# Moving a Q/K piece ahead of the second memory half, regrouping deferred rows around PV, deferring V-row stores, and using free banks at stage two, in a recurrent attention and spatial-gating kernel

## Chip, cores and metric

One core of a Trainium2 chip. The metric is device time in microseconds (us), lower is better. The runs of one kernel spread by up to 0.9% here, so small effects are read from distances inside a trace; the best of these repeat to about 0.002 us. With one core there is no second die to compare, so a run counts as fast unless it is over 1.5% above the fastest of its kernel.

Engines: PE is TensorE, ACT is ScalarE, DVE is VectorE, POOL is GpSimd, SP issues most DMAs.

## The reference

```python
x = A_x                                   # 2048 rows of 512
h = x + A(layernorm(x), mem0, Wq, Wk, Wv, Wo)   # 64 segments of 32 rows, 8 memory rows
h2 = h + B(layernorm(h), w_in, w_sp, b_sp, w_out)

def A(x, mem, ...):                       # 32 heads of 128
    for s in range(64):
        h = concatenate([mem, x[32*s:32*s+32]])          # 40 rows
        q, k, v = h @ Wq, h @ Wk, h @ Wv                 # per head
        p = softmax(mask(q @ k.T * 128 ** -0.5))
        o = (p @ v) @ Wo                                 # summed over heads
        mem = o[:8]                                      # the next segment needs it
        out.append(o[8:])

def B(x, ...):
    z = gelu(x @ w_in);  z1, z2 = halves(z)
    g = w_sp @ layernorm(z2) + b_sp
    return (z1 * g) @ w_out
```

What matters is the recurrence. The eight memory rows of a segment come out of its output projection, and the next segment's Q, K and V all need them. So 64 segments run one after the other, and anything that lengthens the chain inside a segment is paid 64 times.

## The kernel before

The kernel has three stages: weights arrive and the first projections are made (about 55 us), 64 segments follow (about 620 us), and the dense part B ends it (about 175 us). The change touches all three. Eight of the 32 rows of each segment (here "extra" rows) have their Q, K and V, which do not depend on the memory, computed beforehand in batches and kept. Their output projection is deferred too, as no later segment needs it: the "batched rows" of the change are groups of four such matmuls, taken from a queue and used as filler. (The prediction calls them "deferred memory-row products". That is a slip: the memory rows' own projection cannot be deferred, and `cTx`, which these matmuls read, holds the extra rows. Its argument does not depend on it.)

PSUM has eight banks:

```python
# (half of the heads, first pair, pairs, 0 = Q / 1 = K, PSUM bank)
QKP = ((0, 0, 8, 0, 0), (0, 0, 8, 1, 1), (1, 0, 8, 0, 6), (1, 0, 4, 1, 7), (1, 4, 4, 1, 2))
SB = 5                                  # scores
UBK = (0, 1)                            # softmax sums
PVB = (0, 1, 6, 7)                      # PV
VB = {(0, 0): 6, (1, 0): 7, (1, 2): 2}  # V: its first half goes to bank 6
OB = 2; OB2 = 6                         # output projection, first and second 256 columns
Tst = sb("Tst", [128, 2, 512], BF)      # staging: one slot for Q, one for K

def QK(s, k, dc, first=0, last=3, held=False):   # four matmuls, one per column tile of 32
    b, p0, np_, mi, bank = QKP[k]
    ...
def QK_evac(piece):
    b, p0, np_, mi, bank = piece
    st_ = Tst[:, mi, 64 * p0:64 * (p0 + np_)]
    tok = [("T", mi, k) for k in halves(b, p0, np_)]
    act(... st_ <- ps[:, bank, 0:64 * np_] ..., reads=[PB(bank)], writes=tok)     # ACT copy
    dve(... QT or KT <- transpose(st_) ..., reads=tok, ...)                       # DVE transpose
```

One segment, in the order in which PE gets its work:

```python
QK(s, 0, 0); QK(s, 1, 0, last=2, held=True)
if s > 0:
    mem_out(s - 1, 1)                   # second memory half: columns for dc 2 and 3
QK(s, 0, 1); QK(s, 1, 1, last=2, held=True)
QK(s, 0, 2); QK(s, 0, 3);               QK_evac(QKP[0])    # first piece: Q of heads 0..15
QK(s, 1, 3, last=2, held=True)
QK(s, 1, 2, last=2);                    QK_evac(QKP[1])    # second: K of the same heads
QK(s, 2, 2, first=2, last=0, held=True)
QK(s, 2, 3, first=2, last=0)
QK(s, 2, 1, first=2, last=0)
QK(s, 2, 0, first=2, last=0);           QK_evac(QKP[2])    # third: Q of heads 16..31
...                                                        # fourth and fifth: K of those
S_half(s, 0)                            # scores: needs the first and second piece transposed
sm_exp(0)
for dc in range(DC): V_half(s, 0, (0, 4), dc)              # V, first half, into bank 6
... sm_sums(0) ... S_half(s, 1) ... V_half(s, 1, ...) ... sm_sums(1) ...
nw1, nw2, nw4 = (2, 1, 2, 1)[j4], 0, 1  # fillers: before PV, after PV, at the end; j4 = s % 4
fill(nw1); xs[:2]; PV_half(s, 0); PV_half(s, 1); xs[2:4]; fill(nw2)
Wo(WOQ, OB, 0, OC);     part_evac(s, OB, 0, OC)
Wo(WOQ[:6], OB2, OC, D)
mem_out(s, 0)                           # first memory half: columns for dc 0 and 1
Wo(WOQ[6:], OB2, OC, D); part_evac(s, OB2, OC, D)
fill(nw4)
```

In the first stage each of eight V-row groups of 128 KB goes to memory at once, on the GpSimd queue, while Wk and Wo still arrive on the SP queue:

```python
t, tok = part[:, n, :], ...             # ck == 0
em.add("pool", lambda e: e.dma_start(dst, t...), reads=tok, writes=[("vext", ck, n)], dma=True)
```

At the entry of part B (the change calls it stage two), the last deferred products go to bank 4 (`WXB`), behind F_group in bank 3 (`XB`), and z1 of part B follows.

The softmax here doesn't subtract the row's maximum and nothing guards it: scores larger than these inputs give would overflow.

## Time and profile before

| | before |
|---|---|
| median time, all four runs of the first comparison | 854.16 us (852.58 to 854.69) |
| profiled span | 848.4 us, clock 0.999 |
| first output-projection matmul of segment zero | 54.57 us |
| first memory half ready to start (L722, first) | 57.04 us |
| period of segments without filler | 9.723 us |
| period with filler, odd / even segments, median | 9.724 / 9.751 us |
| last segment's first output-projection matmul | 671.33 us |
| from there to the end | 177.07 us |

The period is the distance from one segment's first output-projection matmul to the next one's. It is the number to watch: 63 periods make 600 us, so 0.1 us in each is 6.3 us.

The prediction shows the lines of this profile that it rests on. In such lines the columns are start, time busy, engine, line, operation, output and input, shape and number, and in brackets how long the engine sat idle and for whom.

```profile
148.11 0.60 ACT L559 ACTIVATE f_Tst<-f_ps 128x512 bf16<-128x512 f32 x1 [0.21 <-PE f_ps L289]
148.86 0.20 PE L601 MATMUL f_ps<-f_QT,f_arena 128*32 128x64 bf16 x4
148.89 1.03 PE L289 MATMUL f_ps<-f_arena,f_hT 128*32 128x512 bf16 x16
```

V (L289, the sixteen matmuls at 148.89) writes bank 6. The same bank holds the third Q/K piece until that ACT copy ends, at 148.71. V follows the last score matmuls (L601) by 0.03 us: it waits for nothing.

The same stretch of segment zero, where no memory has to be waited for and the pieces come bunched, looks different:

```profile
49.09 0.28 PE L595 MATMUL f_ps<-f_QT,f_KT 128*32 128x40 bf16 x16 [0.30 <-DVE f_KT L567]
49.21 0.20 PE L601 MATMUL f_ps<-f_QT,f_arena 128*32 128x64 bf16 x4
49.30 1.05 PE L289 MATMUL f_ps<-f_arena,f_hT 128*32 128x512 bf16 x16
```

Here S waits for the K transpose, and V comes 0.09 us after L601, not 0.03.

### The profile page before, as it was taken

The page shows a single profiled execution, that of the slowest core. Times are in us where ns is not written, and L with a number is a line of the kernel's source. Part 1 is how long each engine was busy: PE and PEld are TensorE (multiplying, and loading weights), DVE is VectorE, ACT ScalarE, POOL GpSimd, SP SyncE. Part 2 cuts the span into 40 slices and gives each one's busy share as a digit, 9 for nine tenths or more (in the row PEclk, how much of TensorE's full clock was granted, in tenths as well). Part 3 has the DMA queues.
Part 4 walks back from the last instruction along what each step waited for, and adds up shares of the span by engine and source line. Part 5 has one row for each costly group of instructions (what it writes and reads, how often), then busy time and mean ns, then how long its engine had stood idle before and what let it go on. Part 6 is the DMA issues. An engine that isn't in the chain of part 4 may idle for free.

```text
span 848.4 us, 46072 instructions
## 1 busy us (share of the span) xinstructions
PE 834.1 (98%) x22552; PEld 438.3 (52%) x19480; DVE 515.3 (61%) x1322; ACT 471.7 (56%) x1367; POOL 168.7 (20%) x425
## 2 busy tenths in 40 slices
PE   8889999999999999999999999999999999999998
PEld 8545555555545555555555555555555544444443
DVE  3456666676666666666766666666666664453443
ACT  3446666766667676667666666767666755300000
POOL 7312212121212122221222121122111232100000
PEclk9999999999999999999999999999999999999999
DMA  9972220222332221322222324242321690033001
GB/s 319 392 231 75 69 74 28 60 72 61 77 92 58 50 66 43 75 38 61 60 73 73 95 57 80 60 94 72 58 52 56 188 280 7 1 112 106 32 12 40
DMA packets 112920, 75.25 MB, mean 89 GB/s; under 512 B 70728, under 2 KB 98512, under 8 KB 112720
## 3 DMA queue, kind: packets, MB, share of 16 engines
q1 hardware_dynamic: 111504, 70.88, 30.2%
q8 instruction: 166, 2.72, 1.3%
q0 software_dynamic: 384, 1.05, 0.3%
q10 hardware_dynamic: 832, 0.33, 0.1%
q14 instruction: 34, 0.28, 0.1%
HBM read 39.46 MB, written 20.58 MB: 71 GB/s over the span
## 4 chain that ended last, share of the span: by engine, by line
PE 92%; SPq 5%; DMA 1%; issue 0%; DVE 0%; ACT 0%
PE f_ps L289 33%; PE f_ps L701 14%; PE f_ps L290 12%; PE f_ps L1172 11%; PE f_ps L751 3%; PE f_ps L666 3%; PE f_ps L1165 3%; PE f_ps L1248 3%; SPq L329 3%; PE f_ps L1129 3%; PE f_ps L498 2%; DMA f_arena<-in_A_Wo_dram 1%; SPq L825 1%; PE f_ps L595 1%; PE f_ps L615 1%; PE f_ps L672 1%
## 5 line engine op out<-in xcount | busy, mean ns | idle before, releaser
L289 PE MATMUL f_ps<-f_arena,f_hT 128*32 128x512 bf16 (+1 forms) x5632 | 359.7, 331 | 0.3
L289 PEld LDWEIGHTS f_ps<-f_arena,f_hT 128*32 128x32 bf16 x5632 | 133.1, 96 | 161.6 <-issue 69.8
L290 PE MATMUL f_ps<-f_arena,f_hT 128*32 128x512 bf16 (+1 forms) x2560 | 188.5, 315 | 0.0
L559 ACT ACTIVATE f_Tst<-f_ps 128x512 bf16<-128x512 f32 (+1 forms) x320 | 149.7, 510 | 57.6 <-PE f_ps L289 53.9
L701 PE MATMUL f_ps<-f_arena,f_cT 128*32 128x256 bf16 x4096 | 130.6, 274 | 0.9 <-DMA f_arena<-in_A_Wo_dram 0.6
L638 POOL TENSOR_TENSOR f_E_sb<-f_R_sb,f_E_sb 128x64 bf16<-128x64 f32 x128 | 57.0, 446 | 362.1 <-ACT f_R_sb L630 362.1
L567 DVE STREAM_TRANSPOSE f_QT<-f_Tst 128x256 uint32<-128x256 uint32 x128 | 57.1, 446 | 94.3 <-ACT f_Tst L559 94.3
L701 PEld LDWEIGHTS f_ps<-f_arena,f_cT 128*32 128x32 bf16 x4096 | 90.0, 94 | 37.1 <-ACT f_cT L686 23.2
L1172 PE MATMUL f_ps<-f_arena 128*128 128x512 bf16 x448 | 100.6, 379 | 0.0
L688 DVE TENSOR_SCALAR f_cT<-f_ps 128x160 bf16<-128x160 f32 x256 | 65.2, 318 | 35.2 <-PE f_ps L672 35.2
L713 ACT ACTIVATE f_part<-f_ps 128x256 bf16<-128x256 f32 x128 | 49.1, 383 | 57.7 <-PE f_ps L701 53.7
L658 DVE TENSOR_SCALAR f_V_sb<-f_ps 128x512 bf16<-128x512 f32 (+1 forms) x128 | 71.1, 555 | 13.6 <-PE f_ps L289 13.6
L686 ACT ACTIVATE f_cT<-f_ps 128x160 bf16<-128x160 f32 x256 | 57.1, 310 | 36.3 <-PE f_ps L672 36.3
L1172 PEld LDWEIGHTS f_ps<-f_arena 128*128 128x128 bf16 x448 | 43.8, 98 | 52.8
L567 DVE STREAM_TRANSPOSE f_KT<-f_Tst 128x128 uint32<-128x128 uint32 (+1 forms) x192 | 65.9, 356 | 2.8
L626 ACT ACTIVATE f_R_sb<-f_ps 128x160 f32<-128x160 f32 x128 | 38.9, 304 | 34.8 <-PE f_ps L290 34.8
L634 DVE TENSOR_TENSOR f_E_sb<-f_R_sb,f_E_sb 128x160 bf16<-128x160 f32 x128 | 41.7, 326 | 23.4 <-ACT f_R_sb L630 23.4
L1178 DVE TENSOR_TENSOR f_arena<-f_ps,f_arena 128x512 f32<-128x512 f32 x28 | 19.3, 690 | 54.4 <-PE f_ps L1172 52.4
L289 PE MATMUL f_ps<-f_arena,f_hTe 128*32 128x512 bf16 x640 | 48.8, 382 | 0.0
L608 ACT ACTIVATE f_E_sb<-f_ps 128x224 bf16<-128x224 f32 x128 | 45.9, 359 | 0.1
L751 PE MATMUL f_ps<-f_arena,f_cTx 128*32 128x512 bf16 x512 | 43.9, 379 | 0.5 <-issue 0.4
L630 ACT ACTIVATE f_R_sb<-f_R_sb 128x160 f32<-128x160 f32 x128 | 42.6, 332 | 2.0
(123 smaller groups left out, 1027.3 us busy)
## 6 DMA issues: line engine op xcount, KB each, us to landing
wT_d<-f_wst SPq DMA_DIRECT2D x32, 256.0 KB
f_arena<-wT_d SPq DMA_DIRECT2D x32, 256.0 KB
f_arena<-in_A_Wv_dram SPq DMA_DIRECT2D x4, 1024.0 KB
f_arena<-in_A_Wk_dram SPq DMA_DIRECT2D x4, 1024.0 KB
f_arena<-in_A_Wo_dram SPq DMA_DIRECT2D x4, 1024.0 KB
f_Vx<-vext_d SPq DMA_DIRECT2D x124, 32.0 KB
f_arena<-in_A_Wq_dram SPq DMA_DIRECT2D x3, 1024.0 KB
vext_d<-f_Vs SPq DMA_DIRECT2D x20, 128.0 KB
```

The costliest lines, as they stand in the source:

```text
L289: return e.matmul(out, lhsT=lhsT, rhs=rhs, start=start, stop=stop, skip_group_check=True, tile_position=pos)
L290: return e.add_instruction(mybir.InstMatmult(name=nc.get_next_instruction_name(), engine=mybir.EngineType.PE, ins=[e.lower_ap(rhs), e.lowe ...
L559: act(lambda e: e.activation(out=st_.rearrange("p (hp i r) -> p hp i r", i=32, r=2), in_=ps[:, bank, 0:64 * np_].rearrange("p (hp r i) -> ...
L567: dve(lambda e: e.transpose(out=dst, in_=src), reads=tok, writes=[(nm, b, k) for k in halves(b, p0, np_)])
L638: pool(lambda e: e.tensor_tensor(out=ev, in0=rv, in1=ev, op=ALU.mult), reads=[("R", b), ("Ex", b)], writes=[("Ex", b)])
L658: dve(lambda e: e.tensor_scalar(out=dst, in0=src, scalar1=VSC, scalar2=None, op0=ALU.mult), reads=[PB(bank)], writes=tok)
L686: act(lambda e: e.activation(out=dst, in_=src, func=ACT.Copy, scale=UNSC), reads=[PB(PVB[c])], writes=tok)
L688: dve(lambda e: e.tensor_scalar(out=dst, in0=src, scalar1=UNSC, scalar2=None, op0=ALU.mult), reads=[PB(PVB[c])], writes=tok)
L701: pe(lambda e, h=h, g=g, i=i, b=b, c=c: e.matmul(ps[32 * g:32 * g + 32, bank, 0:d1 - d0], lhsT=cTh[:, i, 8:40], rhs=w_o[:, h, d0:d1], star ...
L713: act(lambda e: e.activation(out=part[:, s % 8, d0:d1], in_=ps[:, bank, 0:d1 - d0], func=ACT.Copy), reads=[PB(bank)], writes=[("part", s % ...
L751: pe(lambda e, h=h, g=g, i=8 * qr + bg: e.matmul(ps[32 * g:32 * g + 32, WXB, :], lhsT=cTx[:, rb % 2, i, :], rhs=w_o[:, h, :], start=(i < 4 ...
L1172: pe(lambda e: e.matmul(ps[:, bank, 0:TB], lhsT=z2[:, sc, fb * 128:(fb + 1) * 128], rhs=wTb[tb % 2][:, :, sc, :], start=(sc == 0), stop=(s ...
```

## The change

Its intent, in four parts: (1) fewer DMA bytes while the weights arrive: most V rows are stored in segments two and three (counting from one), and segment zero's output projection takes the last quarter of Wo last; (2) two groups of the third Q/K piece, which need only the first memory half, run ahead of the second memory half, so that PE does not wait for it; (3) the filler of the segment's end moves to before and after PV; (4) the deferred products at stage two's entry use banks 1 and 0, which are free.

```diff
 def vx_evac(ck, n, bank, eng="act", q="sp"):                     # (1)
-    if ck == 1 and n < 4: ... hbuf, xo
-    elif ck == 0: t, tok = part[:, n, :], ...
+    if ck == 0: t = (hbuf, xo, Vs, wst2)[n // 2][:, n % 2, :] ...
+    elif ck == 1 and n < 4: ... part[:, (n + 3) % 4 + 4, :] ...
 ...
+    def store(q, p0, p1):
+        em.add(q, lambda e: e.dma_start(dst[p0:p1], src[p0:p1]), reads=tok, dma=True, ...)
+    elif q == "pool": store(q, 0, 32)               # only 32 of 128 partitions at once
+    return lambda: store("sp", 32 if q == "pool" else 0, 128)
 ...
+    for n in (4, 5): stores[0, n]()                 # behind Wo
+    if s == 1: for n in (6, 7, 0, 1, 2, 3): stores[0, n]() ; stores[1, 0]()
+    if s == 2: for n in range(1, 4): stores[1, n]()
 ...
+    if s == 0:                                      # last quarter of Wo used last
+        q0 = [(c, b) for b in range(2) for c in range(4)]
+        for i, d0 in ((0, 0), (1, 0), (0, OC), (1, OC), (2, 0), (2, OC), (3, 0)): Wo(q0[2*i:2*i+2], ...)

-    OB2 = 6                                                       # (2)
+    OB2 = 7
     QK(s, 0, 0); QK(s, 1, 0, last=2, held=True)
+    QK(s, 2, 0, last=3, held=True)
     mem_out(s - 1, 1)
     QK(s, 0, 1); QK(s, 1, 1, last=2, held=True)
+    QK(s, 2, 1, last=3, held=True)
     ...
-    QK(s, 2, 2, first=2, last=0, held=True); QK(s, 2, 3, ...); QK(s, 2, 1, ...); QK(s, 2, 0, ...)
+    QK(s, 2, 2, held=True); QK(s, 2, 3)
     ... (fourth and fifth piece in the order 3, 1, 2, 0 instead of 0, 1, 2, 3)

-    nw1, nw2, nw4 = (2, 1, 2, 1)[j4], 0, 1                        # (3)
+    nw1, nw2, nw4 = 2, (1, 0, 1, 0)[j4], 0

-    F_group(RB - 1, XB); for qr in range(4): WoX_mm(RB - 1, qr)   # (4)
+    for qr in range(4): WoX_mm(RB - 1, qr, bank=1)
+    F_group(RB - 1, 0)
```

More of the change, by code (lines that the diff above doesn't have):

```diff
@@ L246, in fast_path @@
     wst = sb("wst", [128, RB, 64], BF)
+    wst2 = wst[:].rearrange("p r c -> p (r c)").rearrange("p (j f) -> p j f", j=2)
     ident = sb("ident", [128, 128], BF)
@@ L502, in vx_evac @@
     def vx_evac(ck, n, bank, eng="act", q="sp"):
-        if ck == 1 and n < 4:
-            t, tok = (hbuf, xo)[n // 2][:, n % 2, :], [(("h", "xo")[n // 2], n % 2)]
-        elif ck == 0:
-            t, tok = part[:, n, :], [("part", n, 0), ("part", n, 1)]
+        if ck == 0:
+            t = (hbuf, xo, Vs, wst2)[n // 2][:, n % 2, :]
+            tok = [(("h", "xo", "Vs", "wst")[n // 2], n % 2)]
+        elif ck == 1 and n < 4:
+            i = (n + 3) % 4 + 4
+            t, tok = part[:, i, :], [("part", i, 0), ("part", i, 1)]
         else:
@@ L513, in vx_evac @@
         dst = vext_d[ck, n // 4, 2 * (n % 4):2 * (n % 4) + 2, :, :].rearrange("g p f -> p g f")
-        if q is not None:
-            em.add(q, lambda e: e.dma_start(dst, t.rearrange("p (g f) -> p g f", g=2)), reads=tok, writes=[("vext", ck, n)], dma=True)
-        return lambda: sp(lambda e: e.dma_start(dst, t.rearrange("p (g f) -> p g f", g=2)), reads=tok, writes=[("vext", ck, n)])
+        src = t.rearrange("p (g f) -> p g f", g=2)
+        def store(q, p0, p1):
+            em.add(q, lambda e: e.dma_start(dst[p0:p1], src[p0:p1]), reads=tok, dma=True,
+                   writes=[("vext", ck, n, i) for i in range(2) if p0 <= 32 * i < p1])
+        if q == "sp":
+            store(q, 0, 128)
+        elif q == "pool":
+            store(q, 0, 32)
+        return lambda: store("sp", 32 if q == "pool" else 0, 128)
     def load_vx(s, q="sp"):
@@ L522, in load_vx @@
             em.add(q, lambda e, b=b, src=src: e.dma_start(Vx[:, s % NVX, b, :], src),
-                   reads=[("vext", s // CK, n) for n in range(4 * b, 4 * b + 4)], writes=[("Vx", s % NVX, b)], dma=True)
+                   reads=[("vext", s // CK, n, int(s % CK > 3)) for n in range(4 * b, 4 * b + 4)], writes=[("Vx", s % NVX, b)], dma=True)
     QKP = ((0, 0, 8, 0, 0), (0, 0, 8, 1, 1), (1, 0, 8, 0, 6), (1, 0, 4, 1, 7), (1, 4, 4, 1, 2))
@@ L694, in fast_path, with Wo @@
     WOQ = ((0, 0), (2, 0), (0, 1), (2, 1), (1, 0), (3, 0), (1, 1), (3, 1))
-    def Wo(cbs, bank, d0, d1):
+    def Wo(cbs, bank, d0, d1, first=WOQ[0], last=WOQ[-1]):
         for c, b in cbs:
@@ L701, in Wo @@
                 pe(lambda e, h=h, g=g, i=i, b=b, c=c: e.matmul(
-                    ps[32 * g:32 * g + 32, bank, 0:d1 - d0], lhsT=cTh[:, i, 8:40], rhs=w_o[:, h, d0:d1], start=((c, b) == WOQ[0]),
-                    stop=((c, b) == WOQ[-1]), tile_position=(0, 32 * g)),
+                    ps[32 * g:32 * g + 32, bank, 0:d1 - d0], lhsT=cTh[:, i, 8:40], rhs=w_o[:, h, d0:d1], start=((c, b) == first),
+                    stop=((c, b) == last), tile_position=(0, 32 * g)),
                     reads=[("cT", c, b), ("Wo", h // 8)], writes=[PB(bank)])
@@ L745, in load_h, with WoX_mm @@
         sp(lambda e: e.dma_start(hbuf[:, rb % 2, :], xr[:, rb, :]), writes=[("h", rb % 2)])
-    def WoX_mm(rb, qr, bgs=range(8)):
+    def WoX_mm(rb, qr, bgs=range(8), bank=WXB):
         for bg in bgs:
@@ L750, in WoX_mm, with WoX_evac @@
             h = 16 * b + 4 * qr + g
-            pe(lambda e, h=h, g=g, i=8 * qr + bg: e.matmul(ps[32 * g:32 * g + 32, WXB, :], lhsT=cTx[:, rb % 2, i, :], rhs=w_o[:, h, :],
+            pe(lambda e, h=h, g=g, i=8 * qr + bg: e.matmul(ps[32 * g:32 * g + 32, bank, :], lhsT=cTx[:, rb % 2, i, :], rhs=w_o[:, h, :],
                                                            start=(i < 4), stop=(i >= H - 4), tile_position=(0, 32 * g)),
-               reads=[("cTx", rb % 2), ("Wo", h // 8)], writes=[PB(WXB)])
-    def WoX_evac(rb):
-        act(lambda e: e.activation(out=partx[:], in_=ps[:, WXB, :], func=ACT.Copy), reads=[PB(WXB)], writes=["partx"])
+               reads=[("cTx", rb % 2), ("Wo", h // 8)], writes=[PB(bank)])
+    def WoX_evac(rb, bank=WXB):
+        act(lambda e: e.activation(out=partx[:], in_=ps[:, bank, :], func=ACT.Copy), reads=[PB(bank)], writes=["partx"])
     def WoX_scatter(rb, bank):
@@ L794, in wT_piece @@
     def wT_piece(i):
-        sp(lambda e: e.dma_start_transpose(out=wst[:, :, :], in_=B_w_sp[i * 64:(i + 1) * 64, :]), writes=["wst"])
-        sp(lambda e: e.dma_start(wT_d[i], wst[:, :, :]), reads=["wst"], writes=[("wTd", i)])
+        tok = [("wst", 0), ("wst", 1)]
+        sp(lambda e: e.dma_start_transpose(out=wst[:, :, :], in_=B_w_sp[i * 64:(i + 1) * 64, :]), writes=tok)
+        sp(lambda e: e.dma_start(wT_d[i], wst[:, :, :]), reads=tok, writes=[("wTd", i)])
     act(lambda e: e.preload_act_table_set("natural_log_exp_and_others"))
@@ L836, in start_group @@
         return ev(*a, bk, "act" if cnt % 2 == 0 else "dve")
-    stores = []
+    stores = {}
     def start_v(ck, n):
-        if ck == 0:
-            start_group(vx_mm, lambda *a: vx_evac(*a, q="pool"), ck, n)
-        else:
-            stores.append(start_group(vx_mm, lambda *a: vx_evac(*a, q=None), ck, n))
+        stores[ck, n] = start_group(vx_mm, lambda *a: vx_evac(*a, q=None if ck else "pool"), ck, n)
     for i in range(2, 8):
@@ L874, in fast_path @@
         load_vx(j, "act")
-    for f in stores:
-        f()
+    for n in (4, 5):
+        stores[0, n]()
     gx = []
@@ L939, in fast_path @@
             load_h(rb - 1)
+        if s == 1:
+            for n in (6, 7, 0, 1, 2, 3):
+                stores[0, n]()
+            stores[1, 0]()
+        if s == 2:
+            for n in range(1, 4):
+                stores[1, n]()
         if s % 2 == 1 and s // 2 < NWT:
@@ L962, in fast_path @@
         QK_evac(QKP[1])
-        QK(s, 2, 2, first=2, last=0, held=True)
-        QK(s, 2, 3, first=2, last=0)
-        QK(s, 2, 1, first=2, last=0)
-        QK(s, 2, 0, first=2, last=0)
+        QK(s, 2, 2, held=True)
+        QK(s, 2, 3)
         lastop["q"] = em.by_eng["pe"][-1]
         QK_evac(QKP[2])
-        QK(s, 3, 0, held=True)
-        QK(s, 4, 0, last=2, held=True)
-        QK(s, 3, 1)
-        QK(s, 4, 1, last=2, held=True)
-        QK(s, 3, 2)
-        QK(s, 3, 3)
+        QK(s, 3, 3, first=3, last=0, held=True)
+        QK(s, 4, 3, first=3, last=2, held=True)
+        QK(s, 3, 1, first=3, last=0)
+        QK(s, 4, 1, first=3, last=2, held=True)
+        QK(s, 3, 2, first=3, last=0)
+        QK(s, 3, 0, first=3, last=0)
         QK_evac(QKP[3])
-        QK(s, 4, 3, last=2, held=True)
-        QK(s, 4, 2, last=2)
+        QK(s, 4, 0, first=3, last=2, held=True)
+        QK(s, 4, 2, first=3, last=2)
         lastop["k"] = em.by_eng["pe"][-1]
@@ L1051, in fast_path @@
             f()
-        Wo(WOQ, OB, 0, OC)
-        part_evac(s, OB, 0, OC)
-        Wo(WOQ[:6], OB2, OC, D)
+        if s == 0:
+            q0 = [(c, b) for b in range(2) for c in range(4)]
+            for i, d0 in ((0, 0), (1, 0), (0, OC), (1, OC), (2, 0), (2, OC), (3, 0)):
+                Wo(q0[2 * i:2 * i + 2], OB2 if d0 else OB, d0, d0 + OC, q0[0], q0[-1])
+            part_evac(s, OB, 0, OC)
+        else:
+            Wo(WOQ, OB, 0, OC)
+            part_evac(s, OB, 0, OC)
+            Wo(WOQ[:6], OB2, OC, D)
         if s + 1 < NSEG:
@@ L1057, in fast_path @@
             mask_dve()
-        Wo(WOQ[6:], OB2, OC, D)
+        if s == 0:
+            Wo(q0[6:], OB2, OC, D, q0[0], q0[-1])
+        else:
+            Wo(WOQ[6:], OB2, OC, D)
         cTx_copy(s)
@@ L1199, in fast_path @@
         if rb == 0:
-            F_group(RB - 1, XB)
             for qr in range(4):
-                WoX_mm(RB - 1, qr)
+                WoX_mm(RB - 1, qr, bank=1)
+            F_group(RB - 1, 0)
             endA = em.by_eng["pe"][-1]
-            WoX_evac(RB - 1)
+            WoX_evac(RB - 1, 1)
             load_wT(1, [endA])
@@ L1207, in fast_path @@
         if rb == 2:
-            WoX_scatter(RB - 1, XB)
-            F_add(RB - 1, XB)
+            WoX_scatter(RB - 1, 0)
+            F_add(RB - 1, 0)
             h_done(RB - 1)
```

## The prediction

> **What bounds it now.** The clock and the shares come first. The granted clock is full throughout, and the page says that TensorE (PE) is busy for almost the whole span.
>
> ```profile
> PE 834.1 (98%) x22552; PEld 438.3 (52%) x19480; DVE 515.3 (61%) x1322; ACT 471.7 (56%) x1367; POOL 168.7 (20%) x425
> PE 92%; SPq 5%; DMA 1%; issue 0%; DVE 0%; ACT 0%
> ```
>
> Matmul ends are modelled, so 98% does not say that PE has no slack. I therefore read distances from start to start in the timeline of PE. The kernel has three stages: about 55 us in which weights arrive, 64 recurrent segments, and about 175 us of dense work. The segments decide. From the first output-projection matmul (L701) of one segment to that of the next it is 9.72 us in the first four segments, which carry no batched rows (the deferred memory-row products L751, L736, L761). It is also 9.72 to 9.76 us in later ones, which carry two or three groups of four such matmuls of 0.216 us. So 0.4 to 0.6 us of work costs nothing: a dependency chain sets the period, and the batched rows sit in its holes. The two holes are these. First the tail, without filler (segment two) and with it (segment ten):
>
> ```profile
> 76.48 0.21 PE L722 MATMUL f_ps<-f_G_sb,f_part 128*32 128x8 bf16 x8
> 76.55 0.39 PE L701 MATMUL f_ps<-f_arena,f_cT 128*32 128x256 bf16 x8
> 77.00 0.40 PE L289 MATMUL f_ps<-f_arena,f_hT 128*32 128x512 bf16 x4
> ...
> 144.67 0.21 PE L722 MATMUL f_ps<-f_G_sb,f_part 128*32 128x8 bf16 x8
> 144.74 0.39 PE L701 MATMUL f_ps<-f_arena,f_cT 128*32 128x256 bf16 x8
> 144.96 0.39 PE L751 MATMUL f_ps<-f_arena,f_cTx 128*32 128x512 bf16 x4
> 145.19 0.40 PE L289 MATMUL f_ps<-f_arena,f_hT 128*32 128x512 bf16 x4
> ```
>
> From the first memory half (L722) to the first Q/K matmul (L289) it is 0.52 us both times. That is PE latency plus DVE's copy of the memory columns (L728, 0.175 us) plus the hand-over. Eight L701 fill 0.217 us of it; the filler fits the other 0.23 exactly. The second hole lies between the two halves of PV, which wait for DVE's normalisation:
>
> ```profile
> 64.44 0.27 PE L666 MATMUL f_ps<-f_E_sb,f_V_sb 32*128 32x40 bf16 x16 [0.19 <-DVE f_E_sb L634]
> ```
>
> Start to start it is 0.40 us wide without filler, 0.19 with one group before PV (odd segments); with two groups (even ones) it is overrun by 0.03.
>
> In the first stage DMA bounds the start. In the chain of waits, and in PE's timeline:
>
> ```profile
> 39.97 1.96 PE L463 MATMUL f_ps<-f_hTe,f_arena 128*128 128x128 bf16 x32 [0.97 <-DMA f_arena<-in_A_Wk_dram]
> 43.01 2.02 PE L463 MATMUL f_ps<-f_hTe,f_arena 128*128 128x128 bf16 x33 [1.08 <-DMA f_arena<-in_A_Wk_dram]
> 55.73 1.48 PE L701 MATMUL f_ps<-f_arena,f_cT 128*32 128x256 bf16 x45 [0.58 <-DMA f_arena<-in_A_Wo_dram]
> ```
>
> PE waits twice for Wk, then for the last quarter of Wo, which the semaphore record shows landing at 55.69.
>
> **The Trainium skill.** "TensorE: Matmul & The Clock Gate", section "Back-to-back issue gap", gives N/2.4 plus about 2.5 ns, so 216 ns at N = 512; the trace agrees, 0.216 us from one group of four column tiles to the next, whether or not the group reloads its weights. So the two extra groups that keep their weights gain nothing. "TensorEngine Tiling (Array Packing)", section "Key Properties", says that a change of tiling mode drains the engine. That fits the eight 512-column matmuls before PV, which take 0.538 us instead of 0.432; the change keeps the number of such switches. "DMA: Bandwidth & Descriptors", section "Issuing engines are not separate DMA queues", says that all issuers share 16 engines. The trace agrees: a megabyte of weights takes about 2.7 us alone (Wv), but Wk takes up to 3.5 while the GpSimd queue stores V rows. Taking those stores away should therefore help the SP queue.
>
> **The change, part by part.**
>
> (1) V rows. Before, eight stores of 128 KB go out between 25 and 41 us; their packets take 43 us summed over 16 engines, 2.7 us of the DMA system. After, only 32 of 128 partitions go then; the rest waits until Wo is issued or until segments one and two (counted from zero). Three quarters of 2.7 is 2.0 us, by which Wk and Wo should land earlier. The last Wk lands at about 41.0 instead of 42.96; PE needs it at 35.31 + 3 x 1.88 = 40.95, so both waits (2.05 us) vanish. Wo's last quarter lands at about 53.7. The new order in segment zero uses it last: 48 of 64 matmuls run before it, and only eight (0.22) between it and the first memory half. The partial sum then takes 0.2 of PE latency, 0.38 on ACT and a 0.05 hand-over, so the first memory half starts at about 54.6 instead of 57.04. **Gain 2.4 us.** DVE's V copy in segment zero now waits for a store queued behind Wo; the stores behind Wo land 0.35 us after it and then 0.35 apart, so at 54.1, just in time.
>
> (2) Third piece early. Four groups move ahead in the order, none is added. The second memory half's hole (0.247 instead of 0.216 before the first group that needs it) closes: -0.03. But the first Q/K piece now ends after eight groups instead of six, and the second after ten instead of eight. S (L595) needs both transposed:
>
> ```profile
> 146.81 1.08 ACT L559 ACTIVATE f_Tst<-f_ps 128x512 bf16<-128x512 f32 x2 [0.72 <-PE f_ps L289]
> 147.44 0.45 DVE L567 STREAM_TRANSPOSE f_QT<-f_Tst 128x256 uint32<-128x256 uint32 x1 [0.64 <-ACT f_Tst L559]
> 147.93 0.45 DVE L567 STREAM_TRANSPOSE f_KT<-f_Tst 128x256 uint32<-128x256 uint32 x1
> ...
> 148.76 0.27 PE L595 MATMUL f_ps<-f_QT,f_KT 128*32 128x40 bf16 x16
> ```
>
> Today K is ready at 148.38 and S starts at 148.76: 0.38 slack. After, on the same clock of this segment: eight groups end at 146.98; ACT starts 0.225 later, at 147.20, and takes the second piece 0.493 after that, at 147.70 for 0.597; DVE then transposes from 148.32 to 148.77; with a 0.054 hand-over S can start at 148.82, while PE is there at 148.72. **A new stall of 0.10; net +0.07 per segment.** PE is in order, so all behind S shifts: 63 x 0.07 = +4.4 us.
>
> (3) Batched rows around PV. The tail group goes away from every segment that had one, and that hole of 0.23 stays empty, since the third piece too needs the memory columns. Odd segments take two groups before PV instead of one: 0.216 into a hole of 0.19, so +0.015 against today's odd period of 9.72 (that is what today's even ones show). Even segments keep two and get one more between PV and Wo. There the hole is only the wait of the output projection for its copies: 0.467 instead of 0.432 ahead of it, and 1.568 instead of 1.519 for 56 of its matmuls, 0.085 in all. So +0.216 - 0.085 = +0.13. Over 30 odd and 30 even segments: 0.45 + 3.9 = **+4.4 us.**
>
> (4) Free banks at stage two. The deferred products no longer wait for DVE to empty bank 4 (L751 starts at 674.30, with 0.43 of waiting for L741), which could give about 1.5 us. But the first z1 matmuls behind them wait for a weight:
>
> ```profile
> 678.82 1.41 PEld L1165 LDWEIGHTS f_ps<-f_arena 128*128 128x128 bf16 x8 [0.23 <-DMA f_arena<-in_B_w_in_dram]
> ```
>
> This lands at 678.54 either way, as its queue starts from the last segment. PE only gets to the wait sooner. **Gain 0.1.**
>
> Sum: -2.4 + 4.4 + 4.4 - 0.1 = +6.3; 853.65 + 6.3 = 860. I shade it to 859.5, because (2) rests on 0.1 us worked out from four hand-overs.
>
> **Rivals.** (a) The start wins and the loop is neutral: if ACT takes the second piece earlier than 0.493 behind the first, the S stall vanishes, (2) is -0.03 x 63 = -2, and if the filler between PV and Wo is also free, the result is 849. For it: DVE and ACT are only 61% and 56% busy, and someone meant this as a gain. Against it: ACT's spacing of 0.493 is seen in every segment, and the hole before Wo is 0.085, not 0.216. (b) The tail hole is dearer than I think, or the stall at S also delays the last K transposes and the second half of S: I find 0.01 of slack there, so another 0.05 per segment, 863. (c) The stores moved into segments one and two delay the loads of V rows or the w_sp transposes: 1.1 MB over 20 us, where DMA is a quarter busy, so at most a us. (d) The gain at the start is smaller, as DVE's V copy blocks on the store behind Wo, or instruction fetches stall PE (1.16 us of waiting for nothing visible at 53.4 today): it falls to 1 us, giving 861.
>
> **Range and chances.** The start is known to about 1 us, the loop to about 0.07 us per segment (4 us); so 852.5 to 863.5. Gains of over 2% need 17 us, more than all of (1) and (4) at their best; a loss of over 2% needs 0.3 us per segment on top of the start's gain. Faster 0.01, same 0.95, slower 0.04.
>
> **What would show it.** In the timeline after: no wait of L463 for Wk; the first memory half at about 54.6; from memory half to Q/K 0.52 us with only eight matmuls in it; a wait of S for DVE's K transpose of about 0.1 in each segment; periods of about 9.81 (odd) and 9.94 (even); z1 still waiting for w_in. Periods at or below 9.74 would make the prediction wrong, above all if S waits for nothing or the tail hole is filled.

## The result, and the profile after

The changed kernel took 866.15 us in the median of four runs (864.36 to 869.1), against 854.16. The ratio is 1.0147, 95% interval 1.0114 to 1.018. Ratios here are the mean time of one kernel's fast runs over that of the other's fast runs of the same rounds, so not quite the ratio of the medians. The change costs about 12 us; the prediction said 859.5 and 852.5 to 863.5.

| | before | after | predicted for after |
|---|---|---|---|
| profiled span, us | 848.4 | 865.0 | |
| first output projection | 54.57 | 51.00 | |
| first memory half | 57.04 | 56.13 | 54.6 |
| period without filler | 9.723 | 9.866 | about 9.79 |
| period, odd / even, median | 9.724 / 9.751 | 9.873 / 10.072 | 9.81 / 9.94 |
| last output projection to the end | 177.07 | 177.35 | 0.1 less |

In these profiled runs some segments were also longer than the rest of their kind, mostly by stalls of PE for nothing visible: periods that exceed the median by over 0.1 us do so by 2.2 us in all before and 5.4 after. That is part of why the two spans differ by more than the medians. Other profiles of both kinds of kernel have 2.3 to 5.6.

The page's first line for the kernel after, to be held against the one in the prediction:

```profile
PE 845.9 (98%) x22552; PEld 440.9 (51%) x18968; DVE 505.2 (58%) x1322; ACT 464.9 (54%) x1367; POOL 167.0 (19%) x425
```

The number of matmuls is the same, and 512 weight loads are gone. PE's share is again 98%: this view cannot show where 12 us went, as the ends of matmuls are modelled and waits of 0.1 us disappear in it.

**The segment.** First PE's timeline around S in the same segment as before, then ACT's third copy, then DVE's two transposes.

```profile
150.67 0.28 PE L290 MATMUL f_ps<-f_arena,f_hT 128*32 128x256 bf16 x4
150.88 0.28 PE L606 MATMUL f_ps<-f_QT,f_KT 128*32 128x40 bf16 x16
151.00 0.20 PE L612 MATMUL f_ps<-f_QT,f_arena 128*32 128x64 bf16 x4
151.08 1.05 PE L290 MATMUL f_ps<-f_arena,f_hT 128*32 128x512 bf16 x16
```

```profile
150.43 0.60 ACT L570 ACTIVATE f_Tst<-f_ps 128x512 bf16<-128x512 f32 x1
```

```profile
149.89 0.45 DVE L578 STREAM_TRANSPOSE f_QT<-f_Tst 128x256 uint32<-128x256 uint32 x1 [1.03 <-ACT f_Tst L570]
150.38 0.45 DVE L578 STREAM_TRANSPOSE f_KT<-f_Tst 128x256 uint32<-128x256 uint32 x1
```

The last Q/K group (L290, 128x256) starts at 150.67 and lasts 0.11 in the pipeline, so PE is ready for S (L606) at 150.78. S starts at 150.88, 0.05 after the K transpose ends: the stall that the prediction worked out. The waits of PE's weight loads from 70 to 690 us name it, and the kernel before has no such row there (columns: total, times, longest):

```profile
PEld f_ps L606 <- DVE f_KT L578: 13.3, 62, 0.2
```

The total of 13.3 is not the loss. Weight loads run ahead of the matmuls, so each of them waits 0.21, of which PE loses 0.107.

There is a second wait two lines further down. V (151.08) starts 0.085 after L612 (151.00), not 0.03. The profile puts this down to "issue", to nothing that it sees. But the third copy ends at 150.43 + 0.60 = 151.03, and it reads bank 6, which V writes. Over all 64 segments of a profile the distances are these (us, median; range in brackets):

| distance | before, segment zero | before, others | after, all |
|---|---|---|---|
| second copy to third copy, starts | 0.675 | 0.802 | 0.675 (0.673 to 0.676) |
| end of the first piece's transpose to start of the third copy | 0.093 | 0.220 | 0.093 (0.091 to 0.094) |
| end of the third copy to V | 0.053 | 0.184 | 0.053 (0.052 to 0.054) |
| end of the second piece's transpose to S | 0.054 | 0.379 | 0.055 (0.054 to 0.055) |

Such constancy is the mark of a wait. After, V always starts 0.053 us after the third copy's end, and the third copy always 0.093 after the first transpose's end. And in segment zero the kernel before had the same numbers. So far this is read from distances; two experiments below (e4_vbank, e12_stage) test it.

**The end of a segment.** PE's timeline in a segment without filler:

```profile
75.86 0.21 PE L733 MATMUL f_ps<-f_G_sb,f_part 128*32 128x8 bf16 x8
75.92 0.39 PE L712 MATMUL f_ps<-f_arena,f_cT 128*32 128x256 bf16 x8
76.38 0.40 PE L290 MATMUL f_ps<-f_arena,f_hT 128*32 128x512 bf16 x4
```

From memory half to Q/K it is 0.52, with only eight matmuls in between, as predicted. In even segments a filler group (L762) now stands ahead of the output projection (L712), whose copies had let it wait before:

```profile
155.02 0.39 PE L762 MATMUL f_ps<-f_arena,f_cTx 128*32 128x512 bf16 x4
155.24 0.94 PE L712 MATMUL f_ps<-f_arena,f_cT 128*32 128x256 bf16 x28
```

The projection starts 0.22 after the filler group, which is the group's whole length.

**The start.** PE's timeline, and the busy time of the engines in two stretches (columns: window, its length, busy time and instructions of PE, PEld, DVE, ACT, POOL, then granted clock, DMA share, GB/s):

```profile
35.28 7.51 PE L464 MATMUL f_ps<-f_hTe,f_arena 128*128 128x128 bf16 x128
51.00 0.29 PE L712 MATMUL f_ps<-f_arena,f_cT 128*32 128x256 bf16 x3
52.83 2.82 PE L712 MATMUL f_ps<-f_arena,f_cT 128*32 128x256 bf16 x53 [1.54 <-issue]
56.13 0.23 PE L733 MATMUL f_ps<-f_G_sb,f_part 128*32 128x8 bf16 x8 [0.47 <-ACT f_part L724]
```

```profile
51.00:53.00 2.00, 0.46 (x15) 0.27 (x15) 0.73 (x4) 0.54 (x3) 0.40 (x1) 1.00 0.65 202
53.00:56.50 3.50, 3.03 (x69) 2.17 (x61) 0.78 (x2) 0.38 (x1) 0.00 (x0) 0.53 0.22 57
```

The 128 matmuls of L464 run through in 7.51 us: both waits for Wk are gone. Wk's last quarter lands at 40.73 and Wo's at 53.26 (predicted 41.0 and 53.7). But PE stands still from 51.29 to 52.83 for nothing that the profile shows, and then has a granted clock of 0.53: a group of four 256-column matmuls takes 0.213 us instead of 0.109. The Trainium skill, "TensorE: Matmul & The Clock Gate", section "Back-to-back issue gap", gives N/1.2 ns for the cold clock, 213 at N = 256; the trace agrees. So in this profile the start gains 0.9 us instead of 2.4.

**Stage two's entry.** PE's timeline:

```profile
694.53 1.90 PE L1190 MATMUL f_ps<-f_arena 128*128 128x512 bf16 x8 [1.04 <-DMA f_arena<-in_B_w_in_dram]
```

z1 still waits for w_in, now for 1.04 us, and the tail is no shorter: nothing gained, as expected.

### The profile page after: what moved, and what is told of

It is laid out like the page before. It is cut to its first block, busy times and chain, and to the rows that moved or that the text cites. A ratio compares the mean times of both kernels' runs of the same rounds, so it can differ in the third digit from the quotient of the medians.

```text
span 865.0 us, 45558 instructions
## 1 busy us (share of the span) xinstructions
PE 845.9 (98%) x22552; PEld 440.9 (51%) x18968; DVE 505.2 (58%) x1322; ACT 464.9 (54%) x1367; POOL 167.0 (19%) x425
## 4 chain that ended last, share of the span: by engine, by line
PE 93%; DMA 2%; DVE 2%; issue 1%; SPq 1%; ACT 1%; ACTq 0%
PE f_ps L290 30%; PE f_ps L291 15%; PE f_ps L712 12%; PE f_ps L1197 11%; PE f_ps L499 3%; PE f_ps L762 3%; PE f_ps L1190 3%; PE f_ps L1273 3%; PE f_ps L677 2%; PE f_ps L1154 2%; PE f_ps L606 2%; PE f_ps L464 2%; PE f_ps L626 1%; DVE f_hT L739 1%; DMA f_arena<-in_A_Wq_dram 1%
## 5 line engine op out<-in xcount | busy, mean ns | idle before, releaser
L290 PE MATMUL f_ps<-f_arena,f_hT 128*32 128x512 bf16 (+1 forms) x5120 | 335.0, 327 | 3.8
L290 PEld LDWEIGHTS f_ps<-f_arena,f_hT 128*32 128x32 bf16 x5120 | 125.3, 96 | 159.2 <-issue 70.0
L570 ACT ACTIVATE f_Tst<-f_ps 128x512 bf16<-128x512 f32 (+1 forms) x320 | 143.1, 509 | 56.9 <-PE f_ps L290 51.6
L712 PE MATMUL f_ps<-f_arena,f_cT 128*32 128x256 bf16 x4096 | 131.7, 275 | 2.5 <-issue 2.5
L712 PEld LDWEIGHTS f_ps<-f_arena,f_cT 128*32 128x32 bf16 x4096 | 98.2, 96 | 28.6 <-ACT f_cT L697 14.1
L578 DVE STREAM_TRANSPOSE f_KT<-f_Tst 128x128 uint32<-128x128 uint32 (+1 forms) x192 | 60.3, 340 | 2.9
L290 PE MATMUL f_ps<-f_arena,f_hTe 128*32 128x512 bf16 x640 | 49.2, 382 | 0.2 <-issue 0.2
L762 PE MATMUL f_ps<-f_arena,f_cTx 128*32 128x512 bf16 x512 | 41.2, 379 | 0.0
```

The costliest lines, as they stand in the source:

```text
L290: return e.matmul(out, lhsT=lhsT, rhs=rhs, start=start, stop=stop, skip_group_check=True, tile_position=pos)
L570: act(lambda e: e.activation(out=st_.rearrange("p (hp i r) -> p hp i r", i=32, r=2), in_=ps[:, bank, 0:64 * np_].rearrange("p (hp r i) -> ...
L578: dve(lambda e: e.transpose(out=dst, in_=src), reads=tok, writes=[(nm, b, k) for k in halves(b, p0, np_)])
L712: pe(lambda e, h=h, g=g, i=i, b=b, c=c: e.matmul(ps[32 * g:32 * g + 32, bank, 0:d1 - d0], lhsT=cTh[:, i, 8:40], rhs=w_o[:, h, d0:d1], star ...
L762: pe(lambda e, h=h, g=g, i=8 * qr + bg: e.matmul(ps[32 * g:32 * g + 32, bank, :], lhsT=cTx[:, rb % 2, i, :], rhs=w_o[:, h, :], start=(i < ...
```

## The experiments

Twelve kernels ran, each with five rounds beside the kernel before. All gave correct results. "Ratio" is against before of the same rounds, with its 95% interval. The edits are shown cut: lines that are no code give the edit in words, and in e2_third and e6_one the order of the fourth and fifth piece, which changes too, is left out.

| run | median us (range) | ratio | period without filler, odd, even |
|---|---|---|---|
| before, four calls | 852.68, 853.96, 854.29, 853.22 | 1 | 9.723, 9.724, 9.751 |
| after | 866.15 (864.36 to 869.1) | 1.0147 (1.0114 to 1.018) | 9.866, 9.873, 10.072 |
| e1_vrows | 851.31 (848.94 to 852.97) | 0.9969 (0.994 to 0.9998) | 9.724, 9.728, 9.768 |
| e7_stores | 850.59 (849.32 to 852.17) | 0.996 (0.9935 to 0.9985) | 9.720, 9.724, 9.761 |
| e2_third | 862.52 (860.71 to 866.27) | 1.0107 (1.0076 to 1.0138) | 9.866, 9.868, 9.906 |
| e3_rows | 857.93 (856.99 to 858.85) | 1.005 (1.0023 to 1.0077) | 9.724, 9.711, 9.933 |
| e5_entry | 853.87 (851.85 to 858.15) | 1.0001 (0.9971 to 1.0031) | as before |
| e4_vbank | 862.03 (860.64 to 863.57) | 1.0103 (1.0076 to 1.0131) | 9.803, 9.788, 10.010 |
| e12_stage | 860.69 (858.67 to 862.54) | 1.0096 (1.0079 to 1.0112) | 9.804, 9.789, 10.010 |
| e6_one | 853.69 (852.51 to 855.97) | 0.9999 (0.9973 to 1.0025) | 9.727, 9.728, 9.765 |
| e8_best | 851.25 (848.53 to 853.46) | 0.9969 (0.9941 to 0.9997) | 9.724, 9.727, 9.760 |
| e9_extra | 851.51 (848.97 to 854.2) | 0.9978 (0.9955 to 1.0001) | 9.680, 9.682, 9.708 |
| e10_best | 848.7 (845.39 to 850.49) | 0.993 (0.9906 to 0.9954) | 9.678, 9.682, 9.723 |
| e11_after_extra | 854.01 (851.05 to 855.94) | 1.0001 (0.9975 to 1.0027) | 9.680, 9.689, 9.885 |

The theory at the outset: the cost sits in the new Q/K order (stall at S, and a wait of V for bank 6) and in the filler of even segments. The rivals: the filler alone, or the stores moved into segments two and three.

### Each part alone

**e1_vrows**: before with part (1), stores and segment zero's projection order.

```diff
+ store only 32 of 128 partitions at first; the rest behind Wo and in segments one and two
+ if s == 0: output projection in the order q0, last quarter of Wo last
```

> The kernel before with part one alone: the deferred stores of V rows and the output projection of segment zero in the order of the weights' arrival. The prediction as recorded: Wk and Wo land 2 us earlier and the gain is 2.4 us (852 if before is 854). Theory now, from the trace after: the weights do land 2 us or more earlier, but the matmuls of the output projection in segment zero stall for 1.5 us or so on nothing that a semaphore shows, and then run at half the granted clock, so that only 0.5 to 1.2 us are kept (853 to 853.5). If the periods of the later segments stay at 9.72 to 9.76 us, the stores moved into segments one and two cost nothing.

Measured: 851.31, ratio 0.9969, so -2.6 us. PE's timeline:

```profile
52.79 1.90 PE L712 MATMUL f_ps<-f_arena,f_cT 128*32 128x256 bf16 x56
55.16 0.21 PE L733 MATMUL f_ps<-f_G_sb,f_part 128*32 128x8 bf16 x8 [0.47 <-ACT f_part L724]
```

With the full clock the first memory half stands at 55.16, 1.9 earlier than before. The periods are those of before within 0.02, 9.724 and 9.723 in the two segments that now carry the stores, so that rival falls. The lower gain that I expected after seeing the changed kernel's trace (0.5 to 1.2 us) lies inside the interval (0.2 to 5.1) too, but it counted on the half clock of that one profile, which this one does not have.

**e2_third**: before with part (2), the new Q/K order and `OB2 = 7`.

```diff
+ QK(s, 2, 0, last=3, held=True)      # ahead of mem_out(s - 1, 1)
+ QK(s, 2, 1, last=3, held=True)      # behind QK(s, 1, 1, ...)
+ OB2 = 7
```

> The kernel before with part two alone: the third Q/K piece ahead of the second memory half, and the output projection's second half in bank 7. Prediction as recorded: +0.07 us in each of 63 segments, +4.4 us. Theory now: S waits 0.10 us for the transposed K, and the V matmuls behind S wait another 0.06 us because they reuse the bank of the third piece, whose copy by ACT ends later; so the segments take 9.86 to 9.88 us, +0.13 to +0.15 each, +8 to +9 us (862 to 863). Rival: the stalls fall into the hole between the halves of PV and cost nothing, 852 to 854.

Measured: 862.52, ratio 1.0107: +9.1 us, twice the +4.4 of the prediction. The period grows by 0.144, and 63 x 0.144 = 9.1. By the trace this splits into -0.045 (the hole in front of the first group that needs the second memory half), +0.107 (S), +0.057 (V), and 0.023 in small shifts of 0.01.

**e3_rows**: before with part (3).

```diff
- nw1, nw2, nw4 = (2, 1, 2, 1)[j4], 0, 1
+ nw1, nw2, nw4 = 2, (1, 0, 1, 0)[j4], 0
```

> The kernel before with part three alone: no batched rows at the tail of a segment, all of them around PV. Prediction as recorded: odd segments +0.015, even ones +0.13 us, in all +4.4 us. Theory now, from the difference of 0.22 us between even and odd segments of the trace after: odd segments unchanged, even ones +0.18 to +0.21, in all +5.5 to +6.5 us (859.5 to 860.5). The tail from memory half to Q/K stays 0.52 us with only the eight matmuls of the output projection in it. Rival: the rows at the tail delayed the next segment, and moving them is free or a gain (854 or less).

Measured: 857.93, ratio 1.005: +4.3 us. Odd periods change by -0.013, even ones by +0.18, which over 30 of each is +5.0 us; the 5.5 to 6.5 that I expected was a little too much. The even ones pay nearly the whole filler group of 0.216, which now stands between PV and the output projection:

```profile
153.62 0.39 PE L751 MATMUL f_ps<-f_arena,f_cTx 128*32 128x512 bf16 x4
153.84 1.70 PE L701 MATMUL f_ps<-f_arena,f_cT 128*32 128x256 bf16 x56
```

**e5_entry**: before with part (4), banks 1 and 0.

```diff
- F_group(RB - 1, XB); for qr in range(4): WoX_mm(RB - 1, qr)
+ for qr in range(4): WoX_mm(RB - 1, qr, bank=1)
+ F_group(RB - 1, 0)
```

> The kernel before with part four alone: the deferred products of the last rows in banks 1 and 0 at the entry of stage two. Prediction as recorded: gain 0.1 us, since the z1 matmuls behind them wait for w_in; the wait of z1 for that weight grows from 0.2 to 1 us or more, and z1 begins at the same distance (7.2 to 7.5 us) from the first output-projection matmul of the last segment. Rival: the load lands earlier when PE stalls less, and about 1.5 us are gained.

Measured: 853.87, ratio 1.0001. z1 begins 7.57 us after the last segment's projection, 7.49 in before. The free banks gain nothing that this run can show, as z1 waits for its weight. A few tenths are not excluded: from the last segment's first output projection to the end it is 176.9 us in the mean of the six profiled kernels with part (4) (176.3 to 178.2) and 177.8 in the eight without (177.0 to 178.4).

The four alone sum to -2.6 + 9.1 + 4.3 + 0.1 = +10.9; together they cost 12.5 (0.0147 x 854), with an interval of 9.7 to 15.4. The parts add up within that.

### Is it the bank that V waits for?

**e4_vbank**: after, with V's first half in bank 0 and the first softmax sums in bank 6.

```diff
- UBK = (0, 1)
+ UBK = (6, 1)
- VB = {(0, 0): 6, (1, 0): 7, (1, 2): 2}
+ VB = {(0, 0): 0, (1, 0): 7, (1, 2): 2}
```

> The changed kernel with one thing altered: the first half of V goes to bank 0 and the first softmax sums to bank 6, so that V no longer waits for ACT's copy of the third Q/K piece. If the reuse of that bank costs 0.06 us per segment, this is 3 to 4 us faster than the changed kernel (862 to 863), and the gap between S and V shrinks from 0.085 to about 0.03 us. If the wait only takes up time in which something later would have waited anyway, the time stays at 866 and the wait shows up at the sums or at PV.

Measured: 862.03, ratio 1.0103 against 1.0147. PE's timeline around S:

```profile
149.14 0.28 PE L606 MATMUL f_ps<-f_QT,f_KT 128*32 128x40 bf16 x16
149.25 0.20 PE L612 MATMUL f_ps<-f_QT,f_arena 128*32 128x64 bf16 x4
149.28 1.04 PE L290 MATMUL f_ps<-f_arena,f_hT 128*32 128x512 bf16 x16
```

V again follows L612 by 0.03, and starts 0.004 before the third copy ends (median of 64). S still stands 0.055 behind the K transpose. The period falls by 0.063, and 63 x 0.063 = 4.0; the ratios differ by 0.0044, which is 3.8 us. The wait of V for bank 6 is shown.

**e12_stage**: after, with a third staging slot, so that the third copy does not have to wait for the first transpose. There was no room for it, so the initial memory rows share a tile that is not needed until later.

```diff
- Tst = sb("Tst", [128, 2, 512], BF)
+ Tst = sb("Tst", [128, 3, 512], BF)
- st_ = Tst[:, mi, ...];  tok = [("T", mi, k) ...]
+ st_ = Tst[:, mi if mi else 2 * b, ...];  tok = [("T", mi if mi else 2 * b, k) ...]
- m0 = sb("m0", [M, D], BF)
+ m0 = partx[0:M, :]
```

> The changed kernel with a third slot in the staging tile, so that the copy of the third piece no longer shares a slot with the copy of the first. In all 64 segments of the changed kernel the third copy on ScalarE starts 0.091 to 0.094 us after the end of VectorE's transpose of the first piece, 0.675 after the second copy instead of the 0.493 that stands between the first and the second; and V starts 0.053 after the third copy ends. Theory (the third copy waits for its staging slot, and V for the third copy's bank): the third copy starts about 0.49 after the second, V starts 0.02 after the matmul ahead of it instead of 0.075, periods without batched rows fall by 0.05 to 0.06 to about 9.81, as in the run with V in another bank, and the time is near 862.5, a ratio near 1.010. Rival (ScalarE itself takes 0.675, or V waits for something else that comes at the same moment): the periods stay at 9.866 and the time at 866, 1.0147.

Measured: 860.69, ratio 1.0096. The third copy starts 0.477 after the second in every segment, V 0.017 after the matmul ahead of it, and the periods are those of e4_vbank to 0.001. ACT's third copy, and PE's timeline:

```profile
147.38 0.60 ACT L570 ACTIVATE f_Tst<-f_ps 128x512 bf16<-128x512 f32 x1
```

```profile
148.03 0.28 PE L606 MATMUL f_ps<-f_QT,f_KT 128*32 128x40 bf16 x16
148.15 0.20 PE L612 MATMUL f_ps<-f_QT,f_arena 128*32 128x64 bf16 x4
148.18 0.39 PE L290 MATMUL f_ps<-f_arena,f_hT 128*32 128x512 bf16 x4
```

So the chain is shown from both ends. The first piece ends two groups later. Its transpose ends later, which holds the single Q slot of the staging tile. So the third copy starts later, and that holds bank 6, for which V waits. Cutting either link gives the same 0.063 per segment. Only S's own stall is left.

### Can the order be had without the stall?

**e6_one**: before, with one group of the third piece ahead of the second memory half and the others behind the second piece.

```diff
+ QK(s, 2, 0, last=1, held=True)      # ahead of mem_out(s - 1, 1)
- QK(s, 2, 2, ...); QK(s, 2, 3, ...); QK(s, 2, 1, ...); QK(s, 2, 0, ...)
+ QK(s, 2, 2, last=1, held=True); QK(s, 2, 3, last=1); QK(s, 2, 1, last=1)
+ OB2 = 7
```

> The kernel before with the third Q/K piece moved by one group instead of two: one group of it ahead of the second memory half, the others behind the second piece, which then ends after nine groups. Theory: with the second piece ready one group (0.216 us) earlier than in e2_third, S waits for nothing, and ACT's third copy starts when PE lets it, not when ACT lets it, so V waits for nothing either; what is left is the hole at the second memory half, closed: periods 9.68 to 9.70 us without filler at the tail hole, gain 0.03 per segment, 2 us in all (850 to 852 if before is 853). If the cost of e2_third came from having the third piece early as such (held weights, bank 7 for the output projection), this kernel would still lose 4 us or more.

Measured: 853.69, ratio 0.9999: a miss, as I expected 2 us. There is no stall at S (0.163 behind the transpose) or V (0.096 behind the copy). But the hole stayed: the nine groups (36 matmuls) that follow the second memory half take 1.985 us, in e2_third 1.939. The same two groups as before stand between the second memory half and the first group that needs it, so its latency is no better covered. The group ahead only came sooner. It has `OB2 = 7`, held weights and a new order of the last two pieces, as e2_third has, and loses nothing: none of these alone is what part (2) costs.

**e9_extra**: before, with one group of the third piece moved to where the hole is, behind the second memory half.

```diff
 QK(s, 1, 1, last=2, held=True)
+QK(s, 2, 1, first=1, last=0, held=True)
 ...
-QK(s, 2, 2, first=2, ...); QK(s, 2, 3, first=2, ...); QK(s, 2, 1, first=2, ...); QK(s, 2, 0, first=2, ...)
+QK(s, 2, 2, first=1, last=0, held=True); QK(s, 2, 3, first=1, last=0); QK(s, 2, 0, first=1, last=0)
```

> The kernel before with one group of the third Q/K piece put behind the second memory half, where the before kernel has a hole of 0.03 us, and none ahead of it; the second piece ends after nine groups. e6_one missed its gain because its extra group stood ahead of the memory half, so the two groups behind it were the same and the hole stayed. Expected: the hole closes, S and V wait for nothing, periods 9.68 to 9.70 us, gain 1.5 to 2.5 us in all (ratio 0.997 to 0.998). If the period stays at 9.72, something behind S sets it.

Measured: 851.51, ratio 0.9978. The period falls by 0.043 to 9.680: the hole is closed, and S still has 0.163 and V 0.094 to their inputs. At 63 x 0.043 this is 2.7 us; the ratio says 1.9, with an interval that just includes nothing.

**e11_after_extra**: the changed kernel with e9_extra's order, and `OB2 = 6` again.

> The changed kernel with its Q/K order replaced by that of e9_extra, and bank 6 for the output projection again, all else as in the change. If the order alone is to blame for what the change cost beyond the prediction, the 9.1 us of e2_third go and the 2 us of e9_extra come: 866.15 - 11 = 855 (ratio to before 1.001 to 1.003), and the gap of 0.09 us between S and V and the late S are gone from the trace. The even segments keep their extra 0.2 us from the batched rows.

Measured: 854.01, ratio 1.0001. PE's timeline:

```profile
149.15 0.27 PE L606 MATMUL f_ps<-f_QT,f_KT 128*32 128x40 bf16 x16
149.26 0.20 PE L612 MATMUL f_ps<-f_QT,f_arena 128*32 128x64 bf16 x4
149.29 0.60 PE L290 MATMUL f_ps<-f_arena,f_hT 128*32 128x512 bf16 x8
```

Neither wait is there (S stands 0.164 behind the transpose, V 0.093 behind the copy), and 12 us are gone with the Q/K order and the bank that goes with it. Even segments keep 9.885, about 0.2 above odd ones: that is part (3), which here eats what parts (1) and (2) could have given.

### The parts that gain, together

**e7_stores**: before with the stores of part (1) but the old order in segment zero.

```diff
+ store only 32 of 128 partitions at first; the rest behind Wo and in segments one and two
```

> The kernel before with the deferred stores of V rows alone, the output projection of segment zero in its old order. Wo lands at about 53.3 us as in e1_vrows. In the old order 45 matmuls follow the landing and the copy to SBUF is hidden behind 24 of them, so the first memory half comes at 53.3 + 1.35 = 54.6 us; with the new order it came at 55.2, as PE stalled on nothing visible until 52.8 and the copy was no longer hidden (0.47 us of waiting). So the new order adds nothing: equal to e1_vrows within 1 us, perhaps 0.5 faster. The recorded prediction had the order worth about 0.5 us.

Measured: 850.59, ratio 0.996, -3.4 us; the interval overlaps that of e1_vrows. The stores carry the gain, and the special order in segment zero is not shown to be worth anything.

**e8_best**: before with part (1), part (4) and e6_one's order.

```diff
+ the edits of e1_vrows, e5_entry and e6_one
```

> Parts one and four as in the change, the third piece by one group only, the batched rows where they were before. If the parts add up: -2.6 (e1_vrows) - 2 (e6_one) - 0.1, so 848 to 849 if before is 853, a ratio of 0.994 to 0.996.

Measured: 851.25, ratio 0.9969. No better than e1_vrows: a miss that follows from e6_one's, as its order gains nothing (periods of 9.727 and 9.760).

**e10_best**: e7_stores with e9_extra's order.

```diff
+ the edits of e7_stores and e9_extra
```

> e7_stores and e9_extra together: -3.4 and -2 us, ratio 0.993 to 0.995; meant as the version that beats both kernels.

Measured: 848.7, ratio 0.993 (0.9906 to 0.9954). This beats both kernels: 6 us under before, 17 under after. Its two gains are those of e7_stores and e9_extra, whose ratios multiply to 0.9938.

## Why the prediction was wrong, point by point

**The class (same within 2%) and the sign were right, the size was not: +12 us instead of +6.** The bound was read rightly: a chain in each segment sets the period, and PE's 98% does not say so.

**The step that failed is in part (2).** The prediction wrote: "A new stall of 0.10; net +0.07 per segment. PE is in order, so all behind S shifts: 63 x 0.07 = +4.4 us." The stall at S is there with 0.107, the closed hole with -0.045. But the argument took S to be the only reader of what comes later, and let the rest merely shift. V has an input of its own that comes later still. All numbers for it stood in the profile before. On the prediction's clock the first copy starts at 147.20; its transpose begins 0.63 later (146.81 to 147.44 in its own lines) and takes 0.445, so it ends at 148.27. The third copy needs that staging slot: 0.093 later, 148.37, and 0.597 long, 148.96. V needs bank 6: 0.053 later, 149.02. S at 148.82 would let V start at 148.96, 0.14 later. That is a wait of 0.06, and 0.057 was measured. Both hand-overs, 0.093 and 0.053, were in segment zero of the kernel before. This term is worth 4.0 us by the periods, 3.8 and 4.4 by the ratios of e4_vbank and e12_stage, which is most of the 4.7 by which part (2) alone was missed; the rest is small shifts of 0.01 to 0.02 per segment that I have not traced. The sum with V's wait in it would have been 864.

**Rival (b) had the size and the wrong place.** It allowed 0.05 more per segment, but for the last K transposes and the second half of S, and was left out of the sum.

**Part (1), -2.4: right.** e1_vrows gives -2.6 and e7_stores -3.4 (intervals 0.2 to 5.1 and 1.3 to 5.6). The waits for Wk are gone and the landings agree within 0.5 us. In e12_stage, at full clock, the first memory half starts at 54.73, where 54.6 was predicted. In the profiled run of after the lost clock gave back 1.5 of it. Rival (d) foresaw less gain for another cause, DVE's copy or fetching.

**Part (3), +4.4: right in the sum (+4.3), partly by luck.** Odd segments got 0.013 faster instead of 0.015 slower. In even ones I reckoned that 0.085 of the filler's 0.216 would be hidden, and only 0.03 to 0.06 was: the odd estimate was 0.028 too high, the even one 0.05 too low, and over the loop the two errors (0.8 and 1.5 us) partly cancel.

**Part (4), -0.1: not contradicted**, as e5_entry shows nothing measurable. **Rival (a)**, a neutral loop, and **rival (c)**, stores disturbing the segments, fell with e2_third and e1_vrows.

**The range was too narrow.** The loop's uncertainty of 0.07 us per segment was taken around a sum in which one waiter was missing, and shading towards 859.5 went the wrong way.

**What stays open.** The sum of the parts is 10.9 us and the whole 12.5, within the interval. By the medians of the periods there is no gap: three without filler at +0.143, thirty odd ones at +0.149 and thirty even ones at +0.321 make 14.5 us, and the start gives back 2.3 at full clock (57.04 to 54.73), so 12.2. What the runs leave open is the half clock at the start, seen in 5 of the 14 profiles (4 of the 8 kernels with the new stores, 1 of the 6 others); whether the stores make it likelier, and how often it struck the unprofiled runs, can't be said from so few.

## What to carry to other kernels

When work is moved forward in an in-order stream, list everything that reads what now comes later, and also everything that waits for a buffer which those readers hold: here one PSUM bank and one staging slot cost 0.06 us per segment on top of the 0.107 of the data dependency. A stretch of the same kernel where the pieces already come bunched (here segment zero) can show the waits of the new order before it is built. In these runs the hole was closed by one group placed inside it (e9_extra), not by more work ahead of it (e6_one), and filler was free only up to the hole's measured width.

## What the Trainium skill lacked or had wrong

- "PSUM — Partial Sum Buffer", section "PSUM bank collisions raise a hardware error", tells one to guard PSUM by bank and quadrant. It does not say there what the guard costs when the bank comes round. Here it is 0.053 us from the end of ACT's copy to the next matmul into the bank (0.052 to 0.054 in 64 segments), and 0.057 of waiting per segment when the copy is late, 4 us in all.
- "TensorEngine Tiling (Array Packing)", section "PSUM Bottleneck", warns that the PSUM copy may become the bottleneck and advises using both engines. Here neither engine was one (ACT 54%, DVE 58% busy after the change): the copy was late for its staging slot, 0.093 us behind the transpose that freed it. The section does not mention that the copy's destination can hold the bank. And the drain of the section "Key Properties" has no size there: eight 512-column matmuls with a change of mode behind them take 0.538 us instead of 0.432, so about 0.11, with whatever else the switch brings; no run separates the two.
- "TensorE: Matmul & The Clock Gate", section "Back-to-back issue gap": 216 ns by its formula at N = 512 fits (0.216 us from group to group of four column tiles, with or without new weights). Its remark that sustained streams reach about 131 ns at N = 512 is not seen in any run here: between two such matmuls on the full array the distance is never under 0.215 us, in all 14 traces.
- "Runtime: NRT & Kernel Launch", section "Instruction fetch mechanics", calls the cost of crossing an instruction block mostly hidden. In after, PE waited 1.54 us for nothing visible while the last weights arrived (1.16 in before), and two packets on instruction queues end in that stretch, at 51.47 and 51.87, the later one 0.96 before PE goes on. That this is a fetch is an association only; no run here tests it.
